# Attention two runs at a time on a timetable, TensorE in the source's order from the second block on, and x1's operands begun two steps later

## The chip, the cores and the metric

The kernel runs on one core of a Trainium2 chip. A time is the device time of one execution in microseconds (us); of several executions the median counts. The core has a matrix engine (TensorE, PE in the profile, PEld for its weight loads), VectorE (DVE), ScalarE (ACT), GpSimd (POOL) and SyncE (SP), which here only starts transfers. Each engine works through a fixed list of instructions in order. PE writes into eight banks of PSUM, numbered 0 to 7; a bank is 128 partitions by 512 float32.

## What is computed

Windowed attention feeds two layers of feed-forward, all in float32:

```python
B, H, S, D = 4, 8, 576, 64                                # attention
scores = q @ k.T / sqrt(D)                                # a window of 32; for half of the heads with dilation 4
attn = exp(scores - max); attn /= attn.sum() + 1e-9       # masked softmax
x = (attn @ v)                                            # 2304 tokens x 512

h = x @ w_in                                              # 512 -> 2048
x1 = (h * cos(h)) @ w_out                                 # 2048 -> 512

h = maximum(maximum(x1 @ w1, x1 @ w2), x1 @ w3)           # 512 -> 768
out = h @ w_out2                                          # 768 -> 512
```

## The kernel before

**Numbers.** Each float32 operand of a large product is split into a high and a low part, and a product is three passes of PE (high·high, low·high, high·low). So every "chunk" below is three matmuls.

**Blocks and steps.** The 2304 tokens go through the first feed-forward in five blocks of 512, 512, 512, 512 and 256. A block has 16 steps `s`, one for each 128 rows of the hidden layer, numbered on from 0 to 79. A step has eight chunks. Four (kind "h", L359) build `h` of this step in PSUM bank 4 or 5 in turn, reading the attention output from `ring`. Four (kind "a", L408) add `w_out` times `gt` of three steps earlier (`LAG`) to the accumulators in banks 0 to 3. Between them `h` becomes `gt`: ACT or DVE makes `kk` and `r` (L374 or L376 to L388), ACT takes the sine of `r` (L218), DVE multiplies it by `h` (L397, this frees the `h` bank), and the split follows (L140 or L144, L399). In the last step of a block the accumulators are copied to `o` (L418 on DVE, L420 on ACT) and stored as `x1d`.

**Attention.** 48 units (a unit is a pair of heads and 192 queries) give the attention output. `plan[t]` holds the units that block t needs first: 12, 12, 10, 12 and 2 of them; those of `plan[t]` are worked during block t−1. A unit is 8 score matmuls (L269; head 0 into bank 6, head 1 into bank 7), 4 row minima on DVE (L276), 4 exponentials on ACT (L218), the sum and reciprocal (L304, L305), a scaling of all four (L308), 4 transposes on PE into bank 6 (L316, their operand is `e`), a copy to `pt` (L144), 8 output matmuls into bank 7 (L327), and three copies and three subtractions into `ring` (L144, L346). (In the profile the 4 score products of the code are 8 matmuls, since PE takes float32 in two parts; the transposes stay 4.) From the second block on a unit enters at the start of a step, one to a step: scores and exponentials in one step, scaling in the next, transposes and output in the one after. The sine and the exponential need different function tables on ACT, so each group of exponentials costs two table loads; `GROUP` says how many units share them: 2 in the first block, 1 after it.

**Order.** The code issues the instructions in the order of the loop over `s`, and a scheduler, which knows the dependences, sets the final order of each engine's list; it may move a unit's products among the chunks of a step, and split them. Products of one kind on PE that stand together are called a place below; in the steady state each unit has three places (scores, transposes, output), more where it was split.

**Toward the second feed-forward.** In the fourth block's steps 51 to 63 `pre_part` makes operands of `w1`, `w2`, `w3` and stores them (`opd`), a chain over DVE, ACT, POOL and SP. The operands of x1 are made in the last block (steps 64 to 79, k = s − 64): `b_load` brings four quarters `x1raw` for each of two halves c (L608, issued at k = −1 and k = 8), `b_make` forms the differences `bt` (L618) and splits all of them into `ring` (L491 on ACT, L492 on DVE). Their buffers are those of `pre_part` and of the attention's `qkv` loads (five in all). In this last block attention is over, and its products are half as wide (256 tokens).

The loop that sets the entry and the timetable of the operands, word for word:

```python
for t, us in enumerate(plan[1:]):
    for i, u in enumerate(us):
        enter.setdefault(t * NF1 + i * LAST[t] // len(us), []).append(u)
...
        if len(to_exp) >= GROUP[min(t, NBT - 1)] or (to_exp and s % NF1 >= LAST[min(t, len(LAST) - 1)]):
            zt = att_exp(to_exp)
...
        c, n = divmod(k - 2, 8)
        if k >= 2 and n < 6 and c < 2:
```

Of the kernel before, what the change touches and what calls it, by code (L numbers as in the profile page):

```python
# [24 lines left out]
QB = 96  # L25
# [43 lines left out]

LAST = (13, 10, 12, 4)  # L70
GROUP = (2, 1, 1, 1, 1)

# [26 lines left out]
def body(  # L99
# [29 lines left out]
    phase = [0]  # L129
    turn = {}  # L130

    def engine(work):
# [123 lines left out]

    def att_scores(u, n=None):
        b, p, i = u
        places[u] = (6, 7) if n is None else (START[2 * n % len(START)], START[(2 * n + 1) % len(START)])
# [3 lines left out]
        places_of = {}  # L263
        for j, h in HEADS:
            q, k, _ = given[u][j]
            if n is None:
                rows = slice(64 * h, 64 * h + 64)
                sv = bank[6 + h][:QB, j * KB : j * KB + KB]
                nc.tensor.matmul(sv, q[rows], k[rows], start=True, stop=True)  # L269
            else:  # L270
                sv = bank[n % 3][:QB, (2 * j + h) * KB : (2 * j + h + 1) * KB]
                nc.tensor.matmul(sv, q[:, h * QB : (h + 1) * QB], k, start=True, stop=True)  # L272
            places_of[j, h] = sv
# [12 lines left out]
        st[u] = e, m  # L286
# [25 lines left out]
    def att_T(u):  # L312
        e = st[u][0]
        t = bank[places[u][0]][:, : 4 * QB]
        for h in range(4):
            nc.tensor.transpose(t[:, h * QB : (h + 1) * QB], e[:, h, :], ident)  # L316
        pt = ptp.tile([KB, 4, QB], F32, tag="pt", name="pt")
        copy("pt", pt.rearrange("p h q -> p (h q)"), t)
        st[u] = pt

    def att_out(u):
# [4 lines left out]
        for j, h in HEADS:  # L326
            nc.tensor.matmul(  # L327
                o[64 * h : 64 * h + 64, j * QB : (j + 1) * QB],
                vs[j][2][:, 64 * h : 64 * h + 64],
                pt[:, 2 * j + h, :],  # L330
                start=True,
                stop=True,
            )
        x = ring[p]
# [19 lines left out]
    def h_chunks(hv, w, c0, n_tok):  # L354


        def chunk(n, c):
            for j, (a, x) in enumerate(PASSES):
                nc.tensor.matmul(  # L359
                    hv,  # L360
                    w[:, a, 128 * c : 128 * c + 128],
                    ring[c][:, x, c0 : c0 + n_tok],
                    start=n == 0 and j == 0,
                    stop=n == NC - 1 and j == 2,
                )

        return chunk
# [36 lines left out]
    def acc_chunk(t0, first, last, w, gt, dm):  # L404
        n_tok = gt.shape[-1]
        a_dm = acc[dm][:, :n_tok]
        for n, (a, x) in enumerate(PASSES):
            nc.tensor.matmul(  # L408
                a_dm,
                w[:, a, 128 * dm : 128 * dm + 128],  # L410
                gt[:, x, :],
                start=first and n == 0,
                stop=last and n == 2,
            )
        if last:
# [188 lines left out]
    def b_load(t, c):  # L604
        for name, k, n in (("11", 0, 0), ("12", 0, 1), ("22", 1, 1), ("21", 1, 0)):
            x = ip.tile([128, HALF], F32, tag="qkv", name="x1raw")
            t0 = (2 * t + n) * HALF
            nc.sync.dma_start(out=x, in_=x1d[2 * k + c, :, t0 : t0 + HALF])  # L608
            braw["B" + name] = x

    def b_make(c, names, keep=None):

        of = {"T1": ("B12", "B11"), "T2": ("B22", "T1"), "T3": ("B22", "B12"), "T4": ("B21", "T2")}
        for name in names:
            if name in of:
                x, y = of[name]
                out = keep or sp.tile([128, HALF], F32, tag="e", name="bt")
                nc.vector.tensor_tensor(out=out, in0=braw[x], in1=braw[y], op=ALU.subtract)  # L618
                braw[name] = out
            if keep is None:  # L620
                split(b_op(name, c), braw[name], nc.vector)

# [89 lines left out]
    def ff2_early(k):  # L712
# [3 lines left out]
        if k in (-1, 8):  # L716
            b_load(0, (k + 1) // 9)
        c, n = divmod(k - 2, 8)
        if k >= 2 and n < 6 and c < 2:

# [150 lines left out]
    enter = {}  # L871
    for t, us in enumerate(plan[1:]):
        for i, u in enumerate(us):
            enter.setdefault(t * NF1 + i * LAST[t] // len(us), []).append(u)
    to_exp, to_norm, to_out = [], [], []
    NS = NBT * NF1
    PRE_AT = NS - 2 * NF1 + 3
    hvs = {}
    for s in range(NS + LAG):
# [28 lines left out]
        for j, (kind, x, c) in enumerate(chunks):  # L908
# [34 lines left out]
        to_norm = []  # L943
        if len(to_exp) >= GROUP[min(t, NBT - 1)] or (to_exp and s % NF1 >= LAST[min(t, len(LAST) - 1)]):
            zt = att_exp(to_exp)
# [86 lines left out]
```

## Time and profile before

| | |
|---|---|
| three executions, median | 820.23 us (818.51 to 821.61) |
| profiled execution, time | 826.75 us |
| its span in the trace | 824.9 us |
| mean granted clock of PE | 0.979 |
| PE busy | 794.4 us (96%) |
| PE weight loads busy | 681.5 us (83%) |
| DVE busy | 549.7 us (67%) |
| ACT busy | 463.2 us (56%) |
| POOL busy | 117.1 us (14%) |

Step 16 starts at 169.73 us of the span, step 32 at 280.67, step 48 at 395.71, step 64 at 487.04, and the products of the second feed-forward begin near 550. In a row of the timeline the columns are start, duration, engine, line, operation, output<-inputs, tile of PE, shape and the number of instructions put together in the row; a bracket gives the idle time before it and what ended it. A sum over rows overstates PE slightly, since matmuls overlap at their ends; the distance between two starts does not.

### The profile page before, as it was taken

To read this page: it belongs to the slowest core of one execution; us is meant where nothing else is said; L and a number is where in the kernel's file an instruction comes from. 1 tells how busy PE (TensorE), PEld (TensorE's weight loads), DVE (VectorE), ACT (ScalarE), POOL (GpSimd) and SP (SyncE) were. 2 spreads that over 40 slices of the span, in tenths; PEclk is the share of its full clock that TensorE was granted. 3 is DMA by queue.
4 is the path that set the end of the run, shared out by engine and by line. 5 is a ranking of instruction groups with operands and counts; after the bars stand their busy time and mean duration, and the time that the engine had idled before them with its cause. 6 is when DMAs were issued, how large, how long until landed. Compare 5 with 4: busy or idle time off the path is not lost.

```text
span 824.9 us, 13094 instructions
## 1 busy us (share of the span) xinstructions
PE 794.4 (96%) x4484; PEld 681.5 (83%) x4484; DVE 549.7 (67%) x1454; ACT 463.2 (56%) x1063; POOL 117.1 (14%) x106
## 2 busy tenths in 40 slices
PE   7878899999999999999999998999999999999998
PEld 6655677777777777777778887999999999999997
DVE  5888789768886688887577778875563355515540
ACT  5778899868884488884465455343342333422321
POOL 1454344510000000000012212200010000000000
PEclk8878999999999999999999998999999999999999
DMA  9954121134344343332045565448783788448802
GB/s 350 419 213 195 32 60 46 58 123 150 124 125 128 110 161 126 117 111 84 14 179 207 192 224 189 169 146 244 242 297 103 218 248 267 156 131 253 250 30 76
DMA packets 60401, 135.44 MB, mean 164 GB/s; under 512 B 6704, under 2 KB 21168, under 8 KB 60336
## 3 DMA queue, kind: packets, MB, share of 16 engines
q1 hardware_dynamic: 60336, 134.62, 48.9%
q8 instruction: 35, 0.57, 0.3%
q14 instruction: 30, 0.25, 0.1%
HBM read 102.35 MB, written 32.24 MB: 163 GB/s over the span
## 4 chain that ended last, share of the span: by engine, by line
PE 70%; DVE 11%; DMA 7%; ACT 5%; issue 3%; POOL 2%; SPq 1%; POOLq 0%; ACTq 0%; DVEq 0%
PE bank L630 24%; PE bank L408 14%; PE bank L359 14%; PE bank L695 9%; PE bank L269 3%; PE bank L327 2%; DMA rawp<-wd 2%; PE bank L316 2%; DMA opd<-hi 2%; PE bank L272 1%; DVE e L308 1%; DVE wx L192 1%; DVE w L189 1%; DVE r L397 1%; ACT r L218 1%
## 5 line engine op out<-in xcount | busy, mean ns | idle before, releaser
L359 PE MATMUL bank<-ring,w 128*128 128x512 f32 (+1 forms) x960 | 237.5, 384 | 5.4 <-DVE r L397 4.0
L408 PE MATMUL bank<-gt,w 128*128 128x512 f32 (+1 forms) x960 | 225.8, 378 | 3.5 <-DVE o L418 1.6
L359 PEld LDWEIGHTS bank<-ring,w 128*128 128x128 f32 x960 | 166.6, 193 | 39.6 <-DVE r L397 5.1
L408 PEld LDWEIGHTS bank<-gt,w 128*128 128x128 f32 x960 | 167.1, 191 | 38.3 <-DVE o L418 2.1
L630 PE MATMUL bank<-ring,wa 128*128 128x384 f32 x1134 | 198.2, 334 | 0.0
L630 PEld LDWEIGHTS bank<-ring,wa 128*128 128x128 f32 x1134 | 196.6, 188 | 0.0
L218 ACT ACT_TABLE_LOAD x62 | 79.5, 1283 | 8.2 <-issue 3.6
L218 ACT ACTIVATE r<-r,hpi 128x512 f32<-128x512 f32 (+1 forms) x80 | 54.5, 681 | 50.1 <-DVE r L388 39.7
L218 ACT ACTIVATE e<-e,m 96x128 f32<-96x128 f32 x192 | 74.7, 390 | 5.4 <-DVE m L276 5.0
L695 PE MATMUL bank<-g,w 128*128 128x384 f32 x432 | 76.3, 334 | 0.0
L695 PEld LDWEIGHTS bank<-g,w 128*128 128x128 f32 x432 | 75.0, 188 | 0.0
L397 DVE TENSOR_TENSOR r<-bank,r 128x512 f32<-128x512 f32 (+1 forms) x80 | 50.5, 631 | 19.3 <-ACT r L218 19.1
L276 DVE CUSTOM_DVE_ANT_0 e<-bank,cs 96x128 f32<-96x128 f32 x192 | 44.9, 282 | 21.8 <-PE bank L272 12.2
L209 POOL TENSOR_TENSOR w<-wx,w 128x512 fp32r<-128x512 f32 x32 | 47.0, 1472 | 53.3 <-ACT w L144 41.3
L646 ACT COPY s<-bank 128x384 f32<-128x384 f32 x54 | 25.8, 479 | 46.8 <-PE bank L630 46.5
L664 DVE TENSOR_TENSOR s<-s,bank 128x384 f32<-128x384 f32 x36 | 19.9, 554 | 45.0 <-PE bank L630 45.0
L140 POOL TENSOR_SCALAR gt<-r 128x512 fp32r<-128x512 f32 x24 | 16.9, 702 | 231.6 <-PE bank L408 134.2
L399 DVE TENSOR_TENSOR gt<-r,gt 128x512 fp32r<-128x512 f32 (+1 forms) x65 | 40.3, 619 | 9.9 <-POOL gt L140 7.6
L269 PEld LDWEIGHTS bank<-qkv 64*96 64x96 f32 x288 | 23.4, 164 | 19.8 <-issue 5.6
L664 DVE TENSOR_TENSOR mx<-s,bank 128x384 f32<-128x384 f32 x18 | 9.9, 552 | 43.4 <-PE bank L630 43.4
L316 PEld LDWEIGHTS bank<-cs,e 96*128 96x128 f32 x192 | 21.0, 146 | 19.3 <-issue 5.0
L269 PE MATMUL bank<-qkv 64*96 64x128 f32 x288 | 34.5, 298 | 2.2 <-DVE m L276 2.2
(75 smaller groups left out, 903.2 us busy)
## 6 DMA issues: line engine op xcount, KB each, us to landing
wa<-opd SPq DMA_DIRECT2D x72, 512.0 KB, 4.6
qkv<-in_qkv SPq DMA_DIRECT2D x36, 336.0 KB, 2.9
wh<-in_w SPq DMA_DIRECT2D x36, 256.0 KB, 2.8
w<-in_w_in SPq DMA_DIRECT2D x16, 512.0 KB, 9.3
w<-in_w_out SPq DMA_DIRECT2D x16, 512.0 KB, 9.8
wa<-opd SPq DMA_DIRECT2D x24, 256.0 KB, 4.2
qkv<-in_qkv SPq DMA_DIRECT2D x12, 432.0 KB, 9.2
wd<-wh SPq DMA_DIRECT2D x36, 128.0 KB, 1.9
```

Of the source, the lines that this page charges most:

```text
L209: tensor("w_lo").tensor_tensor(out=w[:, 1, :], in0=x, in1=w[:, 0, :].bitcast(F32), op=ALU.subtract)
L218: last_table.append(nc.scalar.activation(*args, **kw).ins)
L269: nc.tensor.matmul(sv, q[rows], k[rows], start=True, stop=True)
L276: nc.vector.tensor_tensor_reduce(out=e[:, 2 * j + h, :], in0=places_of[j, h], in1=mask[:, kind, :], scale=-1.0 / math.sqrt(D), scalar=3e38 ...
L316: nc.tensor.transpose(t[:, h * QB : (h + 1) * QB], e[:, h, :], ident)
L359: nc.tensor.matmul(hv, w[:, a, 128 * c : 128 * c + 128], ring[c][:, x, c0 : c0 + n_tok], start=n == 0 and j == 0, stop=n == NC - 1 and j == 2,
L397: nc.vector.tensor_tensor(out=r, in0=hv, in1=r, op=ALU.mult)
L399: tensor("g_lo").tensor_tensor(out=gt[:, 1, :], in0=r, in1=gt[:, 0, :].bitcast(F32), op=ALU.subtract)
L408: nc.tensor.matmul(a_dm, w[:, a, 128 * dm : 128 * dm + 128], gt[:, x, :], start=first and n == 0, stop=last and n == 2,)
L630: nc.tensor.matmul(out, ops[q][a][:, x, 128 * c : 128 * c + 128], b_op(b, c)[:, y], start=first and c == 0 and n == 0, stop=c == 1 and n == 2,
L664: nc.vector.tensor_tensor(out=o, in0=y, in1=x, op=ALU.add)
L695: nc.tensor.matmul(a, wo[2 * f + r][:, x, 128 * dm : 128 * dm + 128], g2[f, r, n][:, y], start=f == 0 and r == 0 and k == 0, stop=f == NF2 ...
```

## The change

Three things are changed.

1. `pe()` pins: in phases 2 and 3 (step 16 on) every PE instruction of the first feed-forward and of attention keeps the place that the code gives it. The products of the second feed-forward are not pinned.
2. The units of `plan[2]`, `plan[3]` and `plan[4]` go in pairs on a timetable counted in chunks (eight to a step): `PAIR = (7, 20, 13, 3)` puts the scores of pair n after chunk 7 + 20n of the block before, both units' transposes 13 chunks later, both units' output products 3 chunks after that. The scores of both units share banks 6 and 7 (different columns); unit k of the pair has transposes and output in bank 6 + k. The 8 exponentials of a pair go together, with one sum and one reciprocal for both.
3. x1's operands begin at k = 4 instead of k = 2 for the first half (one group in each of six steps, k = 4 to 9); the second half stays at k = 10 to 15. `braw` is keyed by the half, since the first half is now still in use when the second is loaded.

The diff, cut to its core:

```diff
-LAST = (13, 10, 12, 4)
-GROUP = (2, 1, 1, 1, 1)
+LAST = 13
+GROUP = 2
+PAIR = (7, 20, 13, 3)
...
+    def pe(ins):
+        if phase[0] > 1:
+            tc.keep_in_program_order(ins)
...
+    def att_products(u, n=None, k=None):
         b, p, i = u
+        if k is not None:
+            places[u] = (6 + k, 6 + k)
+        else:
+            places[u] = (6, 7) if n is None else (START[2 * n % len(START)], START[(2 * n + 1) % len(START)])
...
-                sv = bank[6 + h][:QB, j * KB : j * KB + KB]
-                nc.tensor.matmul(sv, q[rows], k[rows], start=True, stop=True)
+                at = (2 * (k or 0) + j) * KB
+                sv = bank[6 + h][:QB, at : at + KB]
+                pe(nc.tensor.matmul(sv, q[rows], ks[rows], start=True, stop=True))
...
-            braw["B" + name] = x
+            braw[c, "B" + name] = x
...
-        c, n = divmod(k - 2, 8)
-        if k >= 2 and n < 6 and c < 2:
+        c, n = divmod(k - 4, 6)
+        if k >= 4 and c < 2:
...
-    for t, us in enumerate(plan[1:]):
-        for i, u in enumerate(us):
-            enter.setdefault(t * NF1 + i * LAST[t] // len(us), []).append(u)
+    for i, u in enumerate(plan[1]):
+        enter.setdefault(i * LAST // len(plan[1]), []).append(u)
...
+    pairs = []
+    for t, us in enumerate(plan[2:]):
+        first_at, each, to_T, to_o = PAIR
+        for n in range(0, len(us), 2):
+            at_slot = 8 * NF1 * (t + 1) + first_at + n // 2 * each
+            pairs.append((at_slot, "s", us[n : n + 2]))
+            pairs.append((at_slot + to_T, "t", us[n : n + 2]))
+            pairs.append((at_slot + to_T + to_o, "o", us[n : n + 2]))
+    pairs.sort(key=lambda x: x[0])
+
+    def att_pair(kind, us):
+        if kind == "s":
+            found = [att_products(u, None, k) for k, u in enumerate(us)]
+            for u, places_of in zip(us, found):
+                att_min(u, places_of)
+            att_norm(us, att_exp(us), tensor("norm"))
+        else:
+            for u in us:
+                (att_T if kind == "t" else att_done)(u)
...
+            while pairs and pairs[0][0] <= 8 * s + j:
+                att_pair(*pairs.pop(0)[1:])
```

The new wrapper stands around the matmuls and transposes of L269, L316, L327, L359 and L408 (L278, L331, L342, L374 and L423 after).

PE before, in step 20 (second block). `bank_100` is bank 6 and `bank_101` bank 7, `bank_99` an h bank, `bank_94` to `bank_97` the accumulators; each row is a run of matmuls of one line.

```order
L359 MATMUL bank_99<-ring_150,w 128x512 x3
L359 MATMUL bank_99<-ring_151,w 128x512 x3
L359 MATMUL bank_99<-ring_148,w 128x512 x2
L316 MATMUL bank_100<-cs,e 128x96 x4
L359 MATMUL bank_99<-ring_148,w 128x512
L269 MATMUL bank_101<-qkv 96x128 x2
L359 MATMUL bank_99<-ring_149,w 128x512 x3
L408 MATMUL bank_94<-gt,w 128x512 x2
L269 MATMUL bank_100<-qkv 96x128 x2
L408 MATMUL bank_94<-gt,w 128x512
L408 MATMUL bank_95<-gt,w 128x512 x3
L327 MATMUL bank_101<-pt,qkv 64x96 x4
```

PE after, in step 18 of the same block:

```order
L374 MATMUL bank_99<-ring_149,w 128x512 x3
L423 MATMUL bank_94<-gt,w 128x512 x3
L331 MATMUL bank_100<-cs,e 128x96 x4
L331 MATMUL bank_101<-cs,e 128x96 x4
L423 MATMUL bank_95<-gt,w 128x512 x3
L423 MATMUL bank_96<-gt,w 128x512 x3
L423 MATMUL bank_97<-gt,w 128x512 x3
L342 MATMUL bank_100<-pt,qkv 64x96 x4
L342 MATMUL bank_101<-pt,qkv 64x96 x4
L374 MATMUL bank_98<-ring_150,w 128x512 x3
```

Before, one unit's attention products stand at four places in this step, and two chunks are cut by them; after, two units' products stand together, and only between whole chunks.

ACT before, where the fourth block's accumulators are copied (`o` from `bank_94` and `bank_96`); `ring` and `bt`, `x1raw` are operands of x1, `wa` and `raw` those of w1 to w3, `gt` the hidden layer:

```order
L144 CAST gt<-r 128x256
L491 CAST ring_149<-bt 128x384
L491 CAST wa<-raw 128x256
L491 CAST ring_151<-x1raw 128x384
L420 COPY o<-bank_94 128x512
L491 CAST ring_151<-x1raw 128x384
L491 CAST ring_149<-bt 128x384
L420 COPY o<-bank_96 128x512
```

ACT after, at the same copies:

```order
L223 ACTIVATE r<-r,hpi 128x256
L149 CAST gt<-r 128x256
L506 CAST ring_149<-bt 128x384
L506 CAST wa<-raw 128x256
L506 CAST ring_151<-x1raw 128x384
L435 COPY o<-bank_94 128x512
L435 COPY o<-bank_96 128x512
L223 ACTIVATE r<-r,hpi 128x256
```

Before, two casts of x1's operands stand between the two accumulator copies; after, none does, and the casts shown stand ahead of the first copy.

## Rows read from the trace of the kernel before

**Rows 1.** Windows, second to fourth block: length, busy us (count) per engine, clock, DMA.

```profile
169.73:280.67 110.94, 109.98 (x585) 83.58 (x584) 85.72 (x278) 76.49 (x165) 6.63 (x9) 1.00 0.41 127
280.67:395.71 115.04, 113.63 (x625) 85.14 (x624) 89.74 (x291) 85.49 (x185) 5.67 (x8) 1.00 0.36 115
395.71:487.04 91.33, 91.28 (x426) 73.96 (x424) 65.00 (x128) 46.59 (x86) 17.70 (x20) 1.00 0.46 162
```

**Rows 2.** Timeline of PE, one step of the second block without attention.

```profile
264.35 2.88 PE L359 MATMUL bank<-ring,w 128*128 128x512 f32 x12
...
269.79 1.07 PE L359 MATMUL bank<-ring,w 128*128 128x512 f32 x4
```

**Rows 3.** Timeline of PE, a step with one whole unit.

```profile
232.31 0.68 PE L269 MATMUL bank<-qkv 64*96 64x128 f32 x8
232.92 0.98 PE L359 MATMUL bank<-ring,w 128*128 128x512 f32 x3
...
235.22 0.55 PE L327 MATMUL bank<-pt,qkv 128*64 128x96 f32 x8
235.70 1.65 PE L408 MATMUL bank<-gt,w 128*128 128x512 f32 x6
...
237.88 0.49 PE L316 MATMUL bank<-cs,e 96*128 96x96 f32 x4
238.15 1.63 PE L359 MATMUL bank<-ring,w 128*128 128x512 f32 x6
239.71 0.68 PE L269 MATMUL bank<-qkv 64*96 64x128 f32 x8
```

**Rows 4.** Timeline of PE, a step with a split unit (step 20).

```profile
197.63 1.98 PE L359 MATMUL bank<-ring,w 128*128 128x512 f32 x8
...
205.80 1.07 PE L359 MATMUL bank<-ring,w 128*128 128x512 f32 x4
```

**Rows 5.** Timeline of PE, a wait of the transposes.

```profile
252.99 0.52 PE L316 MATMUL bank<-cs,e 96*128 96x96 f32 x4 [0.96 <-DVE e L308]
```

**Rows 6.** Page, part 5 and timelines of ACT and DVE: single operations of a unit.

```profile
L218 ACT ACTIVATE e<-e,m 96x128 f32<-96x128 f32 x192 | 74.7, 390 | 5.4 <-DVE m L276 5.0
L276 DVE CUSTOM_DVE_ANT_0 e<-bank,cs 96x128 f32<-96x128 f32 x192 | 44.9, 282 | 21.8 <-PE bank L272 12.2
...
177.27 1.28 ACT L218 ACT_TABLE_LOAD   x1
178.57 0.40 ACT L218 ACTIVATE e<-e,m 96x128 f32<-96x128 f32 x1
180.78 0.68 DVE L308 TENSOR_TENSOR e<-e,z 96x512 f32<-96x512 f32 x1
183.49 0.56 DVE L144 COPY pt<-bank 128x384 f32<-128x384 f32 x1 [0.42 <-PE bank L316]
```

**Rows 7.** Timeline of PE, steps 66 to 68: the accumulators change from block 4 to 5.

```profile
499.58 1.59 PE L359 MATMUL bank<-ring,w 128*128 128x256 f32 x12
501.52 0.62 PE L408 MATMUL bank<-gt,w 128*128 128x256 f32 x3 [0.35 <-ACT o L420]
...
506.36 1.01 PE L408 MATMUL bank<-gt,w 128*128 128x256 f32 x3 [0.78 <-DVE o L418]
...
511.79 1.59 PE L359 MATMUL bank<-ring,w 128*128 128x256 f32 x12
...
514.66 1.60 PE L359 MATMUL bank<-ring,w 128*128 128x256 f32 x12
```

**Rows 8.** Windows of the same stretch, columns as in the first group.

```profile
505.00:511.00 6.00, 5.22 (x24) 4.93 (x24) 5.03 (x14) 1.96 (x5) 1.27 (x1) 0.50 0.63 225
```

**Rows 9.** Timelines of ACT and POOL: first and last of x1's quarters; POOL before that.

```profile
489.84 0.51 ACT L491 CAST ring<-x1raw 128x384 fp32r<-128x384 f32 x1 [2.25 <-DMA x1raw<-x1d]
...
503.00 0.51 ACT L491 CAST ring<-x1raw 128x384 fp32r<-128x384 f32 x1 [1.53 <-DMA x1raw<-x1d]
...
485.37 0.80 POOL L140 TENSOR_SCALAR gt<-r 128x512 fp32r<-128x512 f32 x1
```

More of the change, by code (lines that the diff above doesn't have):

```diff
@@ L257, in att_scores, with att_min @@
     def att_scores(u, n=None):
+        att_min(u, att_products(u, n))
+    def att_products(u, n=None, k=None):
         b, p, i = u
-        places[u] = (6, 7) if n is None else (START[2 * n % len(START)], START[(2 * n + 1) % len(START)])
+        if k is not None:
+            places[u] = (6 + k, 6 + k)
+        else:
+            places[u] = (6, 7) if n is None else (START[2 * n % len(START)], START[(2 * n + 1) % len(START)])
+        places_of = {}
+        for j, h in HEADS:
+            q, ks, _ = given[u][j]
+            if n is None:
+                rows = slice(64 * h, 64 * h + 64)
+                at = (2 * (k or 0) + j) * KB
+                sv = bank[6 + h][:QB, at : at + KB]
+                pe(nc.tensor.matmul(sv, q[rows], ks[rows], start=True, stop=True))
+            else:
+                sv = bank[n % 3][:QB, (2 * j + h) * KB : (2 * j + h + 1) * KB]
+                nc.tensor.matmul(sv, q[:, h * QB : (h + 1) * QB], ks, start=True, stop=True)
+            places_of[j, h] = sv
+        return places_of
+    def att_min(u, places_of):
+        b, p, i = u
         e = sp.tile([QB, 4, KB], F32, tag="e", name="e")
         m = smp.tile([QB, 4], F32, tag="m", name="m")
[L263 to L267, printed above, removed]
-                sv = bank[6 + h][:QB, j * KB : j * KB + KB]
-                nc.tensor.matmul(sv, q[rows], k[rows], start=True, stop=True)
[L270 to L273, printed above, removed]
         for j, h in HEADS:
@@ L315, in att_T @@
         for h in range(4):
-            nc.tensor.transpose(t[:, h * QB : (h + 1) * QB], e[:, h, :], ident)
+            pe(nc.tensor.transpose(t[:, h * QB : (h + 1) * QB], e[:, h, :], ident))
         pt = ptp.tile([KB, 4, QB], F32, tag="pt", name="pt")
@@ L326, in att_out @@
         for j, h in HEADS:
-            nc.tensor.matmul(
+            pe(nc.tensor.matmul(
                 o[64 * h : 64 * h + 64, j * QB : (j + 1) * QB],
@@ L332, in att_out @@
                 stop=True,
-            )
+            ))
         x = ring[p]
@@ L358, in chunk @@
             for j, (a, x) in enumerate(PASSES):
-                nc.tensor.matmul(
+                pe(nc.tensor.matmul(
                     hv,
@@ L364, in chunk @@
                     stop=n == NC - 1 and j == 2,
-                )
+                ))
         return chunk
@@ L407, in acc_chunk @@
         for n, (a, x) in enumerate(PASSES):
-            nc.tensor.matmul(
+            pe(nc.tensor.matmul(
                 a_dm,
@@ L413, in acc_chunk @@
                 stop=last and n == 2,
-            )
+            ))
         if last:
@@ L617, in b_make @@
                 out = keep or sp.tile([128, HALF], F32, tag="e", name="bt")
-                nc.vector.tensor_tensor(out=out, in0=braw[x], in1=braw[y], op=ALU.subtract)
-                braw[name] = out
+                nc.vector.tensor_tensor(out=out, in0=braw[c, x], in1=braw[c, y], op=ALU.subtract)
+                braw[c, name] = out
             if keep is None:
-                split(b_op(name, c), braw[name], nc.vector)
+                split(b_op(name, c), braw[c, name], nc.vector)
     bank_of = lambda q: {"X": bank[4 + q % 2], "V": bank[6], "Y": bank[7]}
@@ L943, in body @@
         to_norm = []
-        if len(to_exp) >= GROUP[min(t, NBT - 1)] or (to_exp and s % NF1 >= LAST[min(t, len(LAST) - 1)]):
+        if len(to_exp) >= GROUP or (to_exp and s >= LAST):
             zt = att_exp(to_exp)
```

1 line of the change is left out of this document (added).

## The prediction

> **What bounds the kernel now.** I read the share of busy time first: PE is busy for 96% of the span, so a gain has to shorten PE's own list or one of its few gaps. The change leaves the first 16 steps and the second feed-forward as they are on PE, so I looked at the three blocks in which attention runs beside the first feed-forward, and at the change of accumulators behind them. The windows of these blocks [rows 1] are to be read for length and PE time: 110.94, 115.04 and 91.33 us, with PE idle for 0.96, 1.41 and 0.05. The reader is to see that PE is full at its upper clock (1.00, its 2.4 GHz), while DVE (85.72 of 110.94, 89.74 of 115.04) is the next engine and ACT stands behind it. What attention costs there is found by subtraction: a step without it goes from 264.35 to 269.79 [rows 2], 5.44 us, or 0.68 for each of its eight chunks and 0.227 for a matmul. Sixteen such steps are 87.04; the blocks are longer by 23.90 (10 units), 28.00 (12 units) and 4.29 (2 units), together **56.2 us for 24 units**, 2.34 each.
>
> **What one unit costs, and why.** In a step with a whole unit the starts of the scores go from 232.31 to 239.71 [rows 3], 7.40, so the unit costs 7.40 − 5.44 = 1.96. Its pieces by the distance to the next row: scores 0.61, output 0.48, transposes 0.27, together 1.36. The remaining 0.60 belongs to none of them: it is lost at the three places where PE goes from the wide products to the short ones and back, 0.20 a place. A unit whose scores are split stands in the step from 197.63 to 205.80 [rows 4], 8.17, so it costs 2.73, or 0.77 more; by the order about 7 of the 24 units are split so. 17 × 1.96 + 7 × 2.73 = 52.4, with the idle 2.4 of [rows 1] 54.8, against 56.2 found: the two ways agree to 1.4, which other cuts into chunks take.
>
> **1. Pairs and pinning, on PE.** The change keeps all matmuls. It takes away places: a pair has three, where two units had six to eight, and nothing is cut. Pair: 16 scores 1.22, 8 transposes 0.55, 16 output matmuls 0.96, three places 0.60: 3.33. That the bare pieces double is read from the rows of one unit; whether a place keeps its 0.20 with twice the length no row shows. Its bounds are none of it (2.73) and twice 0.20 (3.93, the place belongs to the unit); I take 0.20, since a whole score group of 8 lost no more than an output group of 8. Twelve pairs: 40.0 (32.8 to 47.2). Against 56.2 this is a gain of **16.2 before waits**.
>
> **2. Waits that the timetable makes.** A pair has three meeting points. (a) Its transposes come 13 chunks, 8.84 us, after its scores. On the way to the first transpose lie a row minimum 0.28, eight exponentials 8 × 0.39 = 3.12, and for the second unit two scalings 2 × 0.68 [rows 6], some 4.8 without the two short operations on the sum: about 4 us in hand. That holds for the pairs that begin at chunk 7, 47 and 87. Those at 27, 67 and 107 begin right behind the last h chunk of a step; in ACT's list the exponentials of such a pair stand behind the `kk`, `r` and sine of this h, and a table load 1.28 [rows 6] follows. That takes the slack to about nothing. There are five such pairs (two in the second block, three in the third). (b) The outputs come 3 chunks, 2.04, after the transposes; two copies of 0.56 [rows 6] lie between: 0.9 in hand, if DVE is free. (c) The next pair's scores come 4 chunks after the outputs and wait for both banks. What a missed meeting costs is bounded by zero and by the longest wait of this kind in the trace, 0.96 [rows 5]. What is queued behind a waiting PE is everything, now that its list is fixed. I take 0.5 for each of the five tight pairs, 2.5, near the 2.4 that the three blocks idle now. **Gain left in the blocks: 16.2 − 2.5 = 13.7, with the 2.4 of today's idle already inside the 56.2.**
>
> **3. ACT and DVE.** Twelve groups of exponentials instead of 24 save 24 table loads of 1.28 [rows 6] on ACT, 30.7 us, and 12 sums and reciprocals on DVE. Both are covered by PE: costed at nothing. But a group is longer: load, eight exponentials, load, 2 × 1.28 + 3.12 = 5.68, and a sine behind it holds the h bank, and with it the h chunks two steps later. From the end of one step's h to the start of the h two steps on PE needs 2 × 5.44 − 2.72 = 8.16; the chain of the sine takes about half of that, and in ACT's list the `kk` and sine that come due stand ahead of the exponentials or a whole step behind them. So nothing is charged. The trace shows the exponential beginning 0.02 after the end of its load (177.27 + 1.28 to 178.57, [rows 6]). The Trainium skill (page "ScalarE: Activation LUTs", section "What ACT_TABLE_LOAD costs") counts a drain of about 1380 ns on top of the 1283 of the load; by that an ACT group would be 3.12 + 2 × 2.66 = 8.4 and the slack of the sine would be gone, and each pair might wait about as long as in the slower case below. The load agrees with the row; the drain after it does not show there.
>
> **4. From block 4 to block 5.** Here PE waits for the accumulators [rows 7]: the two steps from 499.58 to 511.79 take 12.21, where two such steps take 2 × 2.87 (511.79 to 514.66): 6.47 lost. The gaps that end with `o`, four with 0.35 the first and 0.78 the last, 2.84 in all, make less than half of it; behind them the clock falls to 0.50 (its 1.2 GHz) from 505 to 511 [rows 8], after PE had been idle again and again, and that makes the rest. The `o` copies are late because ACT and DVE work on x1's operands first, and those wait for transfers: ACT casts the first `x1raw` at 489.84, 2.8 after the step 64 begins at 487.04, after 2.25 of idling, and the last at 503.00, after 1.53 [rows 9]; the copies stand between these casts. The change says "two steps later", but the order after shows that the scheduler still draws eleven of ACT's twelve casts ahead of the first copy (nine before). What does move: the last attention work of the fourth block ends some three steps into it, two steps sooner by the order, its buffers are free sooner, POOL's low parts no longer stand behind a `gt` of 0.80 [rows 9], and the two copies on ACT stand together. I estimate the quarters 2 to 6 us earlier against step 64, which takes the wait to between nothing and half, and a clock that falls for less time or not at all. Bounds: from all of the 6.47 saved to 2.4 more than now (the `gt` of step 62 stands behind four casts in ACT's list). I take **4.4 saved**, the case in which some 2 remain.
>
> **Sum.** 13.7 + 4.4 = 18.1. Against the profiled execution's own 826.75 (its span 824.9 and 1.85 around it) this is 808.6. The profiled execution is 6.5 above the median of 820.23, the saving is the same in both, so **802 us**.
>
> **Rivals.**
> (A) *The change of accumulators stays as it is*, because the operands are not really later in the order and the quarters come no earlier, the edit not doing what it says. For it: the order. Against it: two copies together, POOL's order. Then only 13.7 is gained: 806.5; with 2.4 more lost, 809.
> (B) *One meeting point of each pair is missed* by what a wait costs today [rows 5]: 12 × 0.96 = 11.5 in place of 2.5, 811. For it: DVE is busy for nearly 80% in these blocks and a scaling may queue behind a copy. Against it: all waits of the three blocks together are 2.4 now.
> (C) *The place belongs to the unit, not to the group*: 47.2 in place of 40.0, 809.
> (D) *Slower: the pinned PE waits at all three points.* ACT's long group (5.68) delays the sine, the sine the h bank, DVE comes late to the scaling, and with the list fixed PE has nothing to do instead. Three waits of 0.96 a pair are 34.6 against the 16.2 gained: 820.2 + 18.4 = 838.6, with nothing saved behind. It decides from 1.35 us lost a pair; to be over 0.5% slower it needs 1.7. For it: DVE and ACT are the next engines, and a pair doubles the lumps. Against it: 56.2 already holds 2.4 idle only, ACT loses 30.7 of work and the chain has 4 us in hand in seven of twelve pairs.
>
> **How the numbers follow.** Forecast 0.52 (its own range 798 to 806); A 0.20; B 0.11; C 0.07; D 0.10. The forecast's lower end is a place that costs less in a pair (down to 7.2 less) or a transition saved whole (2.1 less), of which I take about half. The range that leaves no more than 2 in 10 out runs from 797 to 813, which takes in A, B and C with their own ends. A measurement of this kernel can tell about 0.5%, 4.1 us, from no change: below 816.1 it is faster. The forecast, A, B and C end below that, and D is slower, but B together with A (815.6) or half of D's waits end near no change: faster 0.83, same 0.07, slower 0.10.
>
> **What the profile of the changed kernel would show.** Step 16 starts at the same time, near 169.7. The second, third and fourth blocks are near 105, 109 and 90 (87.04 and 5, 6 and 1 pairs at 3.33, and waits): three places to a pair, 3.33 for all of them, and a step without attention still 5.44. PE's idle in these blocks is 2 to 3, its largest waits at transposes, released by the scaling, in pairs that begin behind an h chunk. Table loads fall by about 24. At the change of accumulators the two steps take near 8 instead of 12.2, and the first cast of `x1raw` comes before or at the start of step 64. It would be wrong if waits of the transposes or of the h bank stand in every pair (B, D), if a pair costs 3.9 on PE (C), or if the stretch at the clock 0.50 is as long as before (A).

## The result

The changed kernel takes 808.95 us (median of 4, 807.83 to 810.44) against 820.92 for the kernel before on the same chip (median of 4, 818.51 to 823.17): 12.0 us less, a ratio of 0.9856 with a 95% interval of 0.9823 to 0.9889. That is faster, inside the range, and two thirds of the 18.1 forecast. (A kernel with the same lists of instructions, below, gave 0.9820, 0.9790 to 0.9851, so the two estimates of the gain are 12.0 and 14.8 us.)

The profiled execution of after took 808.95, its median; its span is 807.2. That of before took 826.75, which is 5.8 above its own. So the two traces differ by more than the medians, 17.8 us, and one can say where: 1.0 before step 16, 12.1 in the second to fourth block, 4.5 from step 64 to the second feed-forward, 0.2 behind that.

The rows below are the windows of the second, third and fourth block after, of the two steps in which the accumulators change, and of a stretch behind the longest wait. Columns: window, length, busy us (count) of PE, PEld, DVE, ACT, POOL, granted clock, DMA share, GB/s.

```profile
168.73:275.92 107.19, 104.58 (x585) 83.64 (x584) 82.75 (x264) 63.05 (x154) 7.07 (x9) 0.98 0.41 126
275.92:383.81 107.89, 106.18 (x626) 84.72 (x624) 87.06 (x279) 69.48 (x173) 6.27 (x8) 1.00 0.38 117
383.81:473.92 90.11, 90.11 (x425) 74.16 (x424) 64.23 (x132) 45.66 (x85) 17.55 (x20) 1.00 0.54 188
486.46:494.18 7.72, 6.26 (x50) 5.84 (x48) 6.92 (x18) 3.99 (x9) 1.39 (x2) 1.00 0.78 290
190.00:197.00 7.00, 7.00 (x40) 5.29 (x35) 4.44 (x18) 1.67 (x3) 0.00 (x0) 0.76 0.75 215
```

Against [rows 1] the blocks are shorter by 3.75, 7.15 and 1.22. Of their 305.19 us, 261.12 are the 48 steps at 5.44, 4.3 are waits of PE, and **39.75 is left for the twelve pairs**; before it was 53.77 for the 24 units without waits. The sum had 40.0. ACT's busy time in the second and third block fell from 76 and 85 us to 63 and 69, and the page counts 38 table loads instead of 62. That relief of ACT is not the gain: the waits of PE did not fall, they rose from 2.4 to 4.3.

PE after, where the waits are: the transposes and outputs of the first pair of the second block, and the transposes of the second pair. The bracket is the idle time and what ended it.

```profile
184.32 0.87 PE L331 MATMUL bank<-cs,e 96*128 96x96 f32 x8
184.97 2.33 PE L423 MATMUL bank<-gt,w 128*128 128x512 f32 x9
189.17 1.01 PE L342 MATMUL bank<-pt,qkv 128*64 128x96 f32 x16 [1.87 <-DVE pt L149]
190.12 2.28 PE L374 MATMUL bank<-ring,w 128*128 128x512 f32 x5
...
205.09 0.52 PE L331 MATMUL bank<-cs,e 96*128 96x96 f32 x4 [0.24 <-DVE e L323]
206.11 0.52 PE L331 MATMUL bank<-cs,e 96*128 96x96 f32 x4 [0.49 <-DVE e L323]
```

The long wait, 1.87, is not at the transposes but at the outputs; the first pair of the third block has one of 1.36 at the same point, and a later one has 0.35. The tight pair waits 0.24 and 0.49 at its transposes. No row of an h or of scores has a bracket in these blocks.

PE after, where no wait is near, from the outputs of one pair to the scores of the pair after the next:

```profile
208.65 0.88 PE L342 MATMUL bank<-pt,qkv 128*64 128x96 f32 x16
209.46 3.01 PE L423 MATMUL bank<-gt,w 128*128 128x512 f32 x12
212.41 1.12 PE L278 MATMUL bank<-qkv 64*96 64x128 f32 x16
213.45 3.06 PE L374 MATMUL bank<-ring,w 128*128 128x512 f32 x12
...
222.48 0.82 PE L331 MATMUL bank<-cs,e 96*128 96x96 f32 x8
223.08 2.31 PE L423 MATMUL bank<-gt,w 128*128 128x512 f32 x9
...
229.08 1.12 PE L278 MATMUL bank<-qkv 64*96 64x128 f32 x16
```

The pieces of a pair by the distance to the next row (rounded to 0.01) are scores 1.05, transposes 0.61 and outputs 0.81 (nine of the twelve outputs take 0.81; the three that waited take 0.94), together 2.47. From the scores of one pair to those of the next it is 16.67, which are 20 chunks of 0.68 and **3.07 for an undisturbed pair**; so 0.60 is left for its three places, 0.20 each. Twelve such pairs are 36.8. The other 2.9 of the 39.75 stand around the waits, in rows without a bracket and at a lower clock.

What kept `pt` back at the first pair's outputs is to be read from DVE:

```profile
186.31 0.68 DVE L391 TENSOR_SCALAR kk<-bank 128x512 int32<-128x512 f32 x1
187.03 0.69 DVE L400 SCALAR_TENSOR_TENSOR r<-kk,bank 128x512 f32<-128x512 int32 x1
187.63 0.68 DVE L412 TENSOR_TENSOR r<-bank,r 128x512 f32<-128x512 f32 x1
188.23 0.42 DVE L403 TENSOR_SCALAR r<-r 128x512 f32<-128x512 f32 x1
188.56 1.02 DVE L149 COPY pt<-bank 128x384 f32<-128x384 f32 x2
```

PE goes on from the transposes to the next chunk at 184.97; the copies begin 3.6 later. DVE is never idle in between: it ends an earlier `gt` and two conversions of weights, and then, from 186.31, the whole chain of the next h stands ahead of the copies in its list.

The change of accumulators after, PE first, then ACT's first cast of `x1raw`:

```profile
486.46 1.59 PE L374 MATMUL bank<-ring,w 128*128 128x256 f32 x12
...
488.65 0.98 PE L423 MATMUL bank<-gt,w 128*128 128x256 f32 x6 [0.24 <-DVE o L433]
490.85 0.62 PE L423 MATMUL bank<-gt,w 128*128 128x256 f32 x3 [1.23 <-DVE o L433]
...
494.18 1.60 PE L374 MATMUL bank<-ring,w 128*128 128x256 f32 x12
```

```profile
473.23 0.51 ACT L506 CAST ring<-x1raw 128x384 fp32r<-128x384 f32 x1 [4.57 <-DMA x1raw<-x1d]
```

The two steps take 7.72 where [rows 7] had 12.21, so 1.98 is lost instead of 6.47. The clock stays at 1.00, where [rows 8] had 0.50. The first quarter is cast 0.7 before step 64 begins (473.92); in [rows 9] it was 2.8 behind.

### The profile page after: what moved, and what is told of

Same layout as the page of the kernel before. It is cut to its first block, busy times and chain, and to the rows that moved or that the text cites. A ratio compares the mean times of both kernels' runs of the same rounds, so it can differ in the third digit from the quotient of the medians.

```text
span 807.2 us, 13050 instructions
## 1 busy us (share of the span) xinstructions
PE 775.5 (96%) x4484; PEld 678.0 (84%) x4484; DVE 542.3 (67%) x1430; ACT 432.9 (54%) x1039; POOL 117.7 (15%) x106
## 4 chain that ended last, share of the span: by engine, by line
PE 59%; DVE 17%; DMA 9%; ACT 8%; issue 4%; POOL 2%; SPq 1%; POOLq 0%; ACTq 0%; DVEq 0%
PE bank L645 24%; PE bank L374 10%; PE bank L423 9%; PE bank L710 9%; DMA wh<-in_w 2%; PE bank L342 2%; DMA rawp<-wd 2%; ACT e L223 2%; DMA wd<-wh 2%; PE bank L278 2%; DVE r L412 2%; PE bank L331 1%; DVE wx L197 1%; DVE e L323 1%; PE bank L281 1%
## 5 line engine op out<-in xcount | busy, mean ns | idle before, releaser
L374 PE MATMUL bank<-ring,w 128*128 128x512 f32 (+1 forms) x960 | 227.5, 381 | 5.5 <-DVE r L412 4.3
L423 PE MATMUL bank<-gt,w 128*128 128x512 f32 (+1 forms) x960 | 217.9, 372 | 2.2 <-DVE o L433 1.5
L374 PEld LDWEIGHTS bank<-ring,w 128*128 128x128 f32 x960 | 168.3, 192 | 39.3 <-DVE r L412 4.9
L423 PEld LDWEIGHTS bank<-gt,w 128*128 128x128 f32 x960 | 166.1, 189 | 34.5 <-DVE o L433 1.9
L389 ACT ACTIVATE kk<-bank 128x512 int32<-128x512 f32 x40 | 23.6, 589 | 30.7 <-PE bank L374 30.5
L189 ACT ACTIVATE wh<-wh 128x256 f32<-128x256 f32 x48 | 20.7, 433 | 33.2 <-DMA wh<-in_w 20.9
L223 ACT ACTIVATION_READ_ACCUMULATOR e<-e,m 96x1 f32 x192 | 36.1, 188 | 0.0
```

Source lines behind the costliest of these rows:

```text
L223: last_table.append(nc.scalar.activation(*args, **kw).ins)
L374: pe(nc.tensor.matmul(hv, w[:, a, 128 * c : 128 * c + 128], ring[c][:, x, c0 : c0 + n_tok], start=n == 0 and j == 0, stop=n == NC - 1 and ...
L389: nc.scalar.activation(kk.bitcast(I32), hv, AF.Copy, scale=INV2PI, bias=0.25)
L423: pe(nc.tensor.matmul(a_dm, w[:, a, 128 * dm : 128 * dm + 128], gt[:, x, :], start=first and n == 0, stop=last and n == 2,))
```

## Experiments

Where it says "without waits", the time is the length of the three blocks less the idle time of PE in them and less 48 x 5.44.

### The kernel before once more

No edit. 

> The kernel before, unchanged, looked at once more. Theory: the profiled execution of before (826.75) was a slow draw of its own, because the clock fell to 0.50 behind the change of accumulators, and most executions lose less there; then another execution shows the two steps of that change in 8.5 to 10.5 us instead of 12.21, the three blocks at 111, 115 and 91 as before, and a time of 818 to 823. Rival: the loss there is the same in all executions and the profiled one was slow elsewhere; then the two steps take 12 again.

Median 822.13 of 12 (815.21 to 826.32), ratio to the same kernel measured beside it 1.0007 (0.9976 to 1.0038). The profiled execution took 826.16. Its windows, the second and third block and the two steps (the fourth block is 91.01):

```profile
171.85:281.65 109.80, 109.80 (x585) 83.65 (x584) 84.94 (x278) 76.61 (x165) 6.94 (x9) 1.00 0.41 127
281.65:395.56 113.91, 113.46 (x625) 85.22 (x624) 89.47 (x291) 85.61 (x185) 5.90 (x8) 1.00 0.37 116
...
499.11:511.23 12.12, 9.25 (x50) 8.36 (x48) 9.96 (x24) 5.66 (x13) 2.16 (x2) 0.72 0.71 249
```

The theory falls in its main point: the loss at the change of accumulators, clock and all, is there again (12.12 against 12.21). The executions differ elsewhere. The waits in the blocks were 2.42 in one and 0.45 in the other. Larger is what comes before step 16, which neither kernel changes: it ends at 169.73 and 171.85 in the two executions of before, at 168.73 after, and at 163.7 to 175.9 over the fourteen traces of this study. The clock shows it: over the first 60 us it is 0.83 in the first trace of before, 0.75 in this one and 0.91 in the pinned kernel below, whose step 16 begins at 164.68.

```profile
0.00:60.00 60.00, 49.07 (x306) 38.38 (x307) 41.67 (x174) 40.58 (x147) 22.26 (x21) 0.75 0.79 308
```
```profile
0.00:60.00 60.00, 44.17 (x319) 34.21 (x320) 45.35 (x182) 46.98 (x158) 27.95 (x24) 0.91 0.91 354
```

Over the first 90 us of all fourteen, the lowest clock (0.79) goes with the latest step 16 (175.88) and the highest (0.92) with the earliest (163.71). Behind step 16, where the two kernels differ, the first trace of before took 655.2 us, this one 652.5, and after 638.4.

### x1's operands at the old steps

```diff
-        c, n = divmod(k - 4, 6)
-        if k >= 4 and c < 2:
+        c, n = divmod(k - 2, 8)
+        if k >= 2 and n < 6 and c < 2:
```

> The changed kernel with x1's operands begun at k = 2 again. Theory: the scheduler draws these operations ahead as far as their inputs allow in both, the lists of the engines are the same but for the names of buffers, so the edit does nothing: the time of the changed kernel, 807 to 811, the two steps at the change of accumulators 7.7, the first quarter cast about 0.7 before step 64. Rival: the edit is what moved the quarters; then the two steps take 12 again and the time is about 813.

Median 806.61 of 6 (803.52 to 810.68), ratio 0.9820 (0.9790 to 0.9851); the two steps take 7.78. All engines' lists are those of the changed kernel, but for the number of one buffer. So the third part of the change does nothing: the operands are not begun later, although the title and the source say so, and the two kernels are one and the same measured twice. The second block of this one has nearly the same wait as after, but it is shorter by 1.47, and the clock tells why: behind the wait it stays at 1.00, where after had 0.76.

```profile
167.38:273.10 105.72, 103.11 (x585) 82.66 (x584) 82.93 (x264) 63.05 (x154) 6.43 (x9) 1.00 0.40 127
188.00:195.00 7.00, 7.00 (x52) 5.46 (x49) 5.34 (x21) 2.42 (x5) 0.00 (x0) 1.00 0.76 244
```
```profile
187.65 1.02 PE L342 MATMUL bank<-pt,qkv 128*64 128x96 f32 x16 [1.75 <-DVE pt L149]
```

Its three blocks take 303.67 with 4.22 of waits, so without that fall of the clock the twelve pairs cost 38.33 without waits, 3.19 each. Behind step 16 it took 636.9.

### Attention one step shorter in the fourth block

```diff
-LAST = (13, 10, 12, 4)
+LAST = (13, 10, 12, 2)
```

> The kernel before with one number changed: the second unit of the fourth block enters at step 49 instead of 50, so that attention ends a step sooner; with it POOL's list in steps 51 to 63 becomes that of the changed kernel (both low parts ahead of the gt). Theory: this is what brought x1's quarters sooner; the first cast comes 1 to 4 us sooner against step 64, the two steps at the change of accumulators take 7.5 to 9.5, and the time falls by 2 to 4. Rival: the quarters come as late as before and the time stays at 820, since the saving came from the order of ACT or from PE's pinning.

Median 818.35 of 12, ratio 0.9963 (0.9938 to 0.9989): some 3 us, 0.9 to 5.1, from one number. In its trace it is 55.07 from step 64 to the second feed-forward, where before had 60.27 and the changed kernel has 55.77. The first cast comes 1.1 before step 64 (483.14), and the two steps take 7.36:

```profile
482.09 0.51 ACT L491 CAST ring<-x1raw 128x384 fp32r<-128x384 f32 x1 [3.62 <-DMA x1raw<-x1d]
```
```profile
495.68 1.60 PE L359 MATMUL bank<-ring,w 128*128 128x256 f32 x12
...
503.04 1.60 PE L359 MATMUL bank<-ring,w 128*128 128x256 f32 x12
```

This is the whole of what the changed kernel saves there, without pairs and without pinning. The chain of `pre_part` begins sooner, since attention's last outputs come 24.1 after the start of the block instead of 28.5 (18.5 in the changed kernel), and POOL's second low part follows its first one at once instead of behind a `gt`. Its last low part comes 84.6 after the start of the block instead of 90.4. Its first low part comes only 1.6 sooner (27.2 instead of 28.9), so some 4 of these 5.8 are gained along the chain, where POOL's order is the difference that its rows show. The two were not tried apart.

### Pinning alone

```diff
+    def pe(ins):
+        if phase[0] > 1:
+            tc.keep_in_program_order(ins)
```

around the same matmuls and transposes, in the kernel before. 

> The kernel before with PE's order pinned from step 16 on and nothing else: one unit at a time, no chunk cut, 72 places of attention on PE in the three blocks where the kernel before has 74. Theory by units (a whole unit 1.96, a split one 2.73): 24 x 1.96 = 47.0 instead of 53.8 without idle, so 5 to 7 us less if no wait is added, about 815. Theory by places alone (each costs the same): two fewer, under 1 us, about 820. Rival: the pinned list makes PE wait for transposes; then idle grows from 2.4 and may eat all of it.

Median 819.66 of 12, ratio 0.9991 (0.9966 to 1.0016): nothing. On PE the units got cheaper, 49.4 without waits instead of 53.2 and 53.8 in the two traces of before; but PE now waits 5.0, in two places:

```profile
188.56 0.52 PE L320 MATMUL bank<-cs,e 96*128 96x96 f32 x4 [3.09 <-ACT e L222]
...
299.00 0.52 PE L320 MATMUL bank<-cs,e 96*128 96x96 f32 x4 [1.56 <-DVE e L312]
```

The rival is right. Of the two theories the one by units comes nearer, with 3.7 to 4.3 saved where it had 5 to 7 and the other under 1: PE leaves the wide products 72 times instead of 74, but no unit's scores are cut into one head and the other any more. (A stretch at the clock 0.50 behind the wait of 3.09 is still in the 49.4; the like of it cost after about 1.4.) What is saved and what is waited for cancel.

### Pairs without pinning

```diff
-        if phase[0] > 1:
+        if phase[0] > 9:
```

> The changed kernel with nothing pinned: pairs on the timetable, but the scheduler orders PE. In its list only two pairs' scores are regrouped and three pairs' outputs are cut, 40 places in place of 36. Theory (a score group whose heads do not alternate costs about 0.6 more per unit, a place 0.2 to 0.33): 1 to 3 us more of attention on PE, 808 to 811. Rival (pinning carries the gain): 815 or more.

Median 807.64 of 4, ratio 0.9830 (0.9793 to 0.9867): as fast as the changed kernel. Without waits the pairs cost 41.7, and the waits are 2.2 in place of 4.3. The clock is 0.50 behind a wait of 1.89 (191.0 to 194.2), three pairs' outputs are cut, and the scores of one pair are cut in two. By their single starts, 0.11 apart instead of in twos, the halves are eight of one head and eight of the other:

```profile
196.15 1.11 PE L278 MATMUL bank<-qkv 64*96 64x128 f32 x8
197.19 0.50 PE L423 MATMUL bank<-gt,w 128*128 128x512 f32 x1
197.62 1.11 PE L278 MATMUL bank<-qkv 64*96 64x128 f32 x8
```

Each half takes 1.04, as long as the sixteen of both heads (1.05). So no gain of the pins can be seen in either kernel, and **the pairs carry the gain in the blocks**.

### A price for a place

```diff
-            pairs.append((at_slot + to_T + to_o, "o", us[n : n + 2]))
+            for i, u in enumerate(us[n : n + 2]):
+                pairs.append((at_slot + to_T + to_o + i, "o", [u]))
```

> The changed kernel with the outputs of the two units of a pair in two places, the second unit's one chunk after the first's: 48 places in place of 36, no other work. Theory (a place costs by the change of products, not by the unit): 12 more places add 12 x 0.20 = 2.4 to the attention's 39.7 on PE without idle, up to 12 x 0.27 = 3.2. Rival (the cost belongs to the unit or its matmuls): it stays within 0.5 of 39.7.

```profile
205.82 0.55 PE L342 MATMUL bank<-pt,qkv 128*64 128x96 f32 x8
206.31 0.98 PE L423 MATMUL bank<-gt,w 128*128 128x512 f32 x3
207.21 0.55 PE L342 MATMUL bank<-pt,qkv 128*64 128x96 f32 x8
207.69 2.34 PE L423 MATMUL bank<-gt,w 128*128 128x512 f32 x9
```

The pairs cost 42.34 without waits, at the upper clock throughout the blocks, against 38.33: 4.0 for twelve more places, 0.33 each. That is two things. The chunk between the outputs takes 0.90 instead of 0.68, so the place itself costs 0.22. And the outputs take 0.49 and 0.48, where the sixteen of an undisturbed pair take 0.81 in one piece: 0.16 more. (Three of the twelve had waited in the kernel that this one is put against and took 0.94, so the mean is 0.33 and not 0.38.) So a place costs what the prediction took, by the change of products and not by the unit, and besides, output products of two units are shorter when they stand together. The single execution took 809.88.

### Scores by head

```diff
-        for j, h in HEADS:
+        for j, h in HEADS if n is not None else [(j, h) for h in range(2) for j in range(2)]:
```

> The changed kernel with each unit's score products ordered by head (both of head 0, then both of head 1) instead of alternating. Theory: products of the two heads, which sit on different halves of PE's rows, run side by side when they alternate (two starts 0.01 apart, then 0.10), and one behind the other when they do not (0.11 to 0.19 apart); a pair's scores then take 1.4 to 1.9 instead of 1.05, 4 to 10 us more for twelve pairs. Rival: the order in a group does not matter, the split groups of before cost more by their place alone; the scores stay at 1.05.

```profile
218.18 1.19 PE L278 MATMUL bank<-qkv 64*96 64x128 f32 x16
219.31 0.96 PE L374 MATMUL bank<-ring,w 128*128 128x512 f32 x3
```

The theory falls: eleven of the twelve groups of scores take 1.12 or 1.13 instead of 1.05, some 1 us in all. The order within a group hardly matters. What remains of the idea is in the rows of before: a group of 8 with both heads takes 0.61 (232.31 to 232.92, [rows 3]), and a group of 4 of one head takes as long. In the split unit of [rows 4] the first of the two groups is

```profile
200.13 0.67 PE L269 MATMUL bank<-qkv 64*96 64x128 f32 x4
200.74 0.96 PE L359 MATMUL bank<-ring,w 128*128 128x512 f32 x3
```

and the second, at 202.09, takes 0.61 too. So a cut that leaves one head alone between wide products doubles the time of the scores; the halves of the pair above, 1.04 each, say the same. (The whole took 815.31, with step 16 at 175.88: a slow first stretch, not the edit; behind step 16 it took 637.6.)

### Transposes sooner

```diff
-PAIR = (7, 20, 13, 3)
+PAIR = (7, 20, 11, 5)
```

> The changed kernel with the transposes two chunks sooner and the outputs where they were (PAIR = 7, 20, 11, 5). Theory of the prediction: pairs that begin at chunk 27, 67 and 107 have no slack, so their transposes now wait about 1.4 each (five pairs, some 6 to 7 us idle at transposes), the others none; and the two waits at outputs go. Rival: the tight pairs had slack too, and idle time falls under 4.

The second, fourth and sixth pairs wait at their transposes, 0.39 and 0.30 in the second block and 0.88, 0.78 and 1.07 in the third, 3.4 in all; of the others the first of the second block waits 0.99 and that of the fourth block 0.13. No output waits, one group of scores does (0.46). So it is mainly the tight pairs that the prediction named, but on average they have about 0.7 in hand and not nothing (1.36 was taken away, 0.68 on average is waited for). The single execution took 808.77.

### Outputs later

```diff
-PAIR = (7, 20, 13, 3)
+PAIR = (7, 20, 13, 4)
```

> The changed kernel with the output products one chunk later (PAIR = 7, 20, 13, 4). Theory: its PE waits of 1.87 and 1.36, at the outputs of the first pair of the second and third blocks, are there because the copies to pt stand on DVE behind the multiplication and limits of an h; one chunk, 0.68, more takes them to about 1.2 and 0.7 or lets the scheduler order the copies first and takes them away: 1 to 3 us less idle, 805 to 808. Rival: the copies keep their place behind work that moves with them, or the next pair's scores now wait, and the idle time of the three blocks stays at 4.

Median 811.75 of 4, ratio 0.9876 (0.9836 to 0.9916), nothing gained. The waits at outputs are gone, and idle is 6.4 instead of 4.3: the chunk after the outputs waits for its h bank (3.6 in three places), the next pair's scores, now one chunk nearer, wait for the copies into `ring` (0.9), and three groups of transposes wait 1.6.

```profile
293.95 0.97 PE L374 MATMUL bank<-ring,w 128*128 128x512 f32 x3 [1.30 <-DVE r L412]
...
350.85 0.46 PE L278 MATMUL bank<-qkv 64*96 64x128 f32 x2
351.59 1.11 PE L278 MATMUL bank<-qkv 64*96 64x128 f32 x14 [0.29 <-DVE ring L361]
```

Two starts 0.74 apart in a group that otherwise takes 1.05: part of such a wait stands inside the row of 0.46, and no bracket shows it.

### x1's operands really later

```diff
-    def split(out, x, lo):
-        nc.scalar.copy(out[:, 0], x)
-        lo.tensor_tensor(out=out[:, 1], in0=x, in1=out[:, 0].bitcast(F32), op=ALU.subtract)
+    def split(out, x, lo, keep=lambda ins: ins):
+        keep(nc.scalar.copy(out[:, 0], x))
+        keep(lo.tensor_tensor(out=out[:, 1], in0=x, in1=out[:, 0].bitcast(F32), op=ALU.subtract))
...
-                b_make(c, (("B11", "T1"), ("B21",), ("T2",), ("B22",), ("T4",))[n])
+                b_make(c, (("B11", "T1"), ("B21",), ("T2",), ("B22",), ("T4",))[n], pin=tc.keep_in_program_order)
```

(`b_make` hands its `pin` on to `split` and to its difference.) 

> The changed kernel with the operations that make x1's operands also held to the code's order on ACT and DVE, so that they are really begun at k = 4, behind the copies of the accumulators. Theory: the copies no longer stand behind casts, the two steps at the change of accumulators take 5.8 to 6.3 instead of 7.72, about 1.5 to 2 us less there, and the second feed-forward starts as before: 805 to 808. Rival: the operands then come late for its first products, or their buffers hold the later transfers, and PE waits more than 2 there: 809 to 813.

Median 803.48 of 6 (802.65 to 808.41), ratio 0.9798 (0.9764 to 0.9831). The first cast of `x1raw` now stands behind both copies of `o`, and the two steps take 5.76, the steady 2 x 2.88:

```profile
481.16 0.59 ACT L435 COPY o<-bank 128x512 f32<-128x512 f32 x1
...
482.72 0.57 ACT L435 COPY o<-bank 128x512 f32<-128x512 f32 x1
...
489.70 0.52 ACT L506 CAST ring<-x1raw 128x384 fp32r<-128x384 f32 x1
```
```profile
483.01 1.60 PE L374 MATMUL bank<-ring,w 128*128 128x256 f32 x12
...
488.77 1.60 PE L374 MATMUL bank<-ring,w 128*128 128x256 f32 x12
```

From step 64 to the second feed-forward it is 54.11 instead of 55.77, so nothing comes late behind it. It beats the kernel before clearly; against the changed kernel the trace shows 1.7 saved at this place, while the intervals of the two ratios overlap.

### Both, and the copies on ACT

The edit above together with PAIR = (7, 20, 13, 4): 

> The changed kernel with both edits, outputs one chunk later and x1's operands held to the code's order. Theory: the two savings add, 2.5 to 5 us together, 803 to 806. Rival: either of the two rivals above holds, and the time is 807 or more.

Median 805.88, ratio 0.9821 (0.9785 to 0.9858): the savings do not add, since the first one is none.

The edit above with `pt` copied by ACT:

```diff
-    "pt": ("A", "A", "V", "V"),
+    "pt": ("A", "A", "A", "V"),
```

> The changed kernel with x1's operands held to the code's order, and the copies to pt on ACT in place of DVE. Theory: the waits at the outputs of the first pairs (1.87 and 1.06 there) fall under 1.2 together, the rest is unchanged: 801 to 805 where the kernel without the move gave 803.5. Rival: ACT's copies stand behind sines and exponentials, outputs wait in more pairs, 806 or more.

Median 804.14, ratio 0.9782 (0.9750 to 0.9814), no different from 0.9798. The waits at the first pairs' outputs shrink to 0.48, but idle is 3.80 where it was 3.77; it goes to the outputs of other pairs (0.32, 0.51), as the rival said, to scores (0.71, 0.45) and to the transposes of a tight pair (1.03).

## Why the prediction was right, and where it was not

**1, the pairs on PE: right in size, in part by luck.** 40.0 for twelve pairs were forecast, 39.75 measured, 38.33 where the clock did not fall. The price of a place was right, 0.20 in an undisturbed pair and 0.22 by the direct test, and rival C is out. The bare pieces were mis-sized: two units' products together take 2.47 and not twice one unit's, 2.73, so an undisturbed pair costs 3.07 instead of 3.33. Twelve of them are 3.2 below the 40.0, and 1.5 to 2.9 were lost again around the waits and to the clock, which the sum did not have. The 0.77 of a split unit is no place alone: it is one more place and one more score group of a single head, which takes as long as one of both. The Trainium skill (page "TensorEngine Tiling (Array Packing)", section "Key Properties") says that different tiles of the array can work in parallel. The rows agree: 8 products of two heads, which use different halves of the array's rows, are done in the time of 4 of one.

**2, the waits: the right number of them in doubt, the wrong meeting point.** 2.5 were forecast at the transposes of five tight pairs. Measured 4.3: 0.7 there, 3.6 at outputs, of which 1.87 and 1.36 in the first pairs of two blocks. The step that failed is the 0.9 in hand of meeting point (b), "if DVE is free": it was not, the chain of an h stood ahead of the copies. And a wait had a price that was left out: behind 1.87 the clock fell in some executions, another 1.4. The tight pairs are the right ones, with some 0.7 in hand. Moving the outputs, or the copies, moved the wait to another meeting point; that DVE's order in these blocks is what is left to change is likely by this, but no run held it.

**3, ACT and DVE: right.** Table loads fell by 24, no h waited, D did not come. In ACT's list an exponential still begins 0.01 to 0.02 after its table load (178.27 + 1.28 to 179.56 in after), and the load itself, in most cases, 0.02 after the operation before it. The drain that the Trainium skill counts for a switch (page "ScalarE: Activation LUTs", section "What ACT_TABLE_LOAD costs") shows on neither side of the load in this trace.

**4, the change of accumulators: right in size, 4.4 forecast and 4.5 measured,** and for the reason given: the shorter attention of the fourth block and POOL's order, which alone saved 5.2 there in that trace and some 3 by the medians. That the x1 edit would do nothing there was seen as rival A; it does nothing at all.

**The sum.** 18.1 between the profiled executions was forecast and 17.8 measured. The step that failed is the last: "the saving is the same in both", taken from the median. The profiled execution of before was slow by 5.8, in part by what neither kernel changes and in part by 2 us of waits in the blocks that another execution did not have. With the blocks of that other one (314.7 against 305.2 and 303.7 for the new lists) and 4.4 behind them, the same sum comes to 14 to 15.5. Its trace says the same behind step 16: 652.5 against 638.4 and 636.9. The medians gave 12.0 and 14.8; how much of the rest is chance is not settled.

**What pinning was for stays open** in one respect: neither with units nor with pairs did it change the time by more than the intervals, some 3 us, but it made a waiting time out of a saving on PE each time.

## What to carry to other kernels

Put small products of two units together in one place between whole chunks, and do not cut a group that fills both halves of the array: that was worth some 14 us of PE time here, and pinning the order nothing that could be measured. When an edit says "later", look at whether the scheduler's list moves; here it took a pin on ACT and DVE. When a sum is made from one profiled execution, subtract its own luck before putting it against a median: 2 us of waits came and went between two executions of one kernel, and the start, the same in all, differed by up to 12 us over the traces.

## What the runs showed of the hardware

- The start of the kernel, the same in all, ended between 163.7 and 175.9 us. The granted clock of its first 60 us was 0.75 (step 16 at 171.85), 0.83 (169.73) and 0.91 (164.68); over the first 90 us it went from 0.79 (175.88) to 0.92 (163.71).
- Waits of PE of 1.87 to 1.89 were followed by a stretch at the lower clock in three executions (0.50 of full speed from 190.5 to 193.7 after, 191.0 to 194.2 without pins, 187.0 to 190.0 with x1's operands really later); one of 1.75 in the lists of after and one of 1.88 with the outputs split were not.
- Sixteen score products of two heads take 1.05 in alternating order and 1.12 by head. Of one head alone, four take 0.61 and eight 1.04; eight of both take 0.61.
- Sixteen output products of two units take 0.81 in one piece, and 0.97 in two with a chunk between them. Going from wide products to short ones and back cost about 0.2 beside the products, whether the short group was of one unit or of two.
